# Causal attention computed for four heads at a time in 64-query blocks, instead of two heads in 128-query blocks

## The chip, the cores and the metric

The kernel runs on one core of one Trainium2 chip. The metric is the device time of one execution in microseconds (us). Three timed runs of the kernel before the change took 458.64, 459.05 and 459.47 us; their median, 459.05 us, is the time to compare with.

## The reference

There are 4 batches of 12 heads, 448 positions and head size 64, all in float32. The attention is causal; its output, laid out as rows of 768 channels, is the x of a mixing layer:

```python
scores = scale * np.matmul(q, k.transpose(0, 1, 3, 2))        # scale = 1/8
scores = np.where(mask, -1000000000.0, scores)                # mask: keys after the query
scores = scores - np.max(scores, axis=-1, keepdims=True)
attn = np.exp(scores)
attn = attn / (np.sum(attn, axis=-1, keepdims=True) + 1e-09)
out = np.matmul(attn, v)

theta = x @ w_theta                                            # x: 4 x 448 x 768
zr, zi = x * np.cos(theta), x * np.sin(theta)
y = np.einsum('ts,bsd->btd', w_tok_r, zr) + np.einsum('ts,bsd->btd', w_tok_i, zi)
u = x + y
result = u + np.maximum(u @ w_ch, 0.0)
```

## The kernel before

Attention is done pair by pair: 24 pairs of heads, six to a batch, each by one call of attend. TensorE (PE) computes the scores with the queries as stationary operand, 128 queries at a time. Queries 0 to 383 make three blocks of 128, whose keys reach to 128, 256 and 384. A head has only 64 channels, so the two heads of a pair use the two halves of the PE array's rows at the same time (line 627). The last 64 queries of both heads are put together into one block of 128 stationary columns, with zeros where one head's query meets the other's channels, and multiplied with all 448 keys on the full array (line 614). VectorE (DVE) adds the mask and takes the row's extreme (line 633), ScalarE (ACT) takes exp and the sums (line 636). PE then transposes the weights in 16 blocks of 128 by 128, in five groups of one PSUM bank each (line 671); ACT or DVE copies each group into the tile pt (lines 504 and 506). The product with v runs as two 128-row, 64-column halves of the array, one for each head, in four steps of 448, 320, 192 and 64 queries (line 697). The seven columns of sums of a pair are inverted on DVE, transposed by PE into the bank xo (line 646), copied (line 647), written to HBM and read back spread over 64 partitions (rb); DVE multiplies the product by rb into xT (line 700).

The rest is full-array work: theta (line 749), the sine and cosine of it, the token mixing y (line 828), and a channel product by a scheme with fewer multiplications (line 926). Weights are decoded on the chip first: ACT and DVE turn raw words into float32 (lines 528 to 534), then a rounded part and a rest are stored by a copy (lines 501 to 506) and a subtraction (line 512).

All instructions are put in order ahead of time by a planner (class Plan). Every piece of work has an engine, a duration that the planner assumes, buffers out of rings of fixed size, and a due time; two tables of numbers, SHIFT and PEN, move the due times of single groups of instructions. At each moment the planner gives a free engine the piece that is due first among those whose inputs and buffers are there; turn adds a duration where PE changes between full-array work and work on halves. What it emits is the order of each engine, and engines run strictly in that order, waiting on each other by semaphores. PSUM has eight banks: two of s, two of t, one xo, three of m. All DMAs are issued by SyncE's queue (line 487).

Of the kernel before, what the change touches and what calls it, by code (L numbers as in the profile page):

```python
# [8 lines left out]
F32 = mybir.dt.float32  # L9
# [12 lines left out]
KN = dict(S0=-62237.8965, P0=19471.4322, P1=5606.0978, V=2.9624, TL=1.1607, RL=-85717.1261, SL=3920.8889, SH=90531.9904,  # L22
# [6 lines left out]
          C0=-30018.6467, C1=-154978.281, C2=8845.5904, SW=32591.9015, HL=13, MP=6, PM=6837.6742, MR3=3.9427, WQ=2)  # L29


SHIFT = {2: -279, 3: -584, 4: 210, 5: 775, 6: 6, 7: -41, 8: 17, 9: 443, 10: -218, 11: 111, 12: -69, 13: 4, 14: -100,
# [146 lines left out]
class Plan:  # L179
# [67 lines left out]
    def order(self):  # L247
# [21 lines left out]
        def turn(a, b):  # L269
            if a == b:  # L270
                return 0
            if b == "r":
                return 87 if a == "x" else 288
            if b == "x":
                return 54 if a == "r" else 145
            if a == "r":
                return 120 if b == "t" else 108
# [11 lines left out]
        out = []  # L289
# [845 lines left out]
```

## Time and profile before

| | |
|---|---|
| median of the three timed runs | 459.05 us |
| span of the profiled execution, first to last instruction | 456.9 us |
| PE busy | 445.3 us, 97% |
| DVE busy | 371.5 us, 81% |
| ACT busy | 247.6 us, 54% |
| POOL busy | 47.0 us, 10% |
| TensorE clock granted, mean | 0.999 of full speed |

The profiled execution is known by its span alone; what lies around the span in a timed run is taken as the difference to the median, 2.15 us. A matmul's duration in the rows includes the time it takes to pass through the array, during which the next one already runs, so the price of a group of matmuls is read from its start to the start of the next group, not from its busy time. A float32 matmul stands as two records. PEld is the load of the stationary operand.

### The profile page before, as it was taken

The page shows a single profiled execution, that of the slowest core. Times are in us where ns is not written, and L with a number is a line of the kernel's source. Part 1 is how long each engine was busy: PE and PEld are TensorE (multiplying, and loading weights), DVE is VectorE, ACT ScalarE, POOL GpSimd, SP SyncE. Part 2 cuts the span into 40 slices and gives each one's busy share as a digit, 9 for nine tenths or more (in the row PEclk, how much of TensorE's full clock was granted, in tenths as well). Part 3 has the DMA queues.
Part 4 walks back from the last instruction along what each step waited for, and adds up shares of the span by engine and source line. Part 5 has one row for each costly group of instructions (what it writes and reads, how often), then busy time and mean ns, then how long its engine had stood idle before and what let it go on. Part 6 is the DMA issues. An engine that isn't in the chain of part 4 may idle for free.

```text
span 456.9 us, 7721 instructions
## 1 busy us (share of the span) xinstructions
PE 445.3 (97%) x2651; PEld 367.1 (80%) x2651; DVE 371.5 (81%) x974; ACT 247.6 (54%) x617; POOL 47.0 (10%) x46
## 2 busy tenths in 40 slices
PE   8988999999999999999999999999999999999996
PEld 3655566877777778898878898889999988998995
DVE  4999999869978878547988846987657999888796
ACT  5988878668796665327984214971134542212320
POOL 1213000000000001000000000030011330242330
PEclk9999999999999999999999999999999999999999
DMA  8877655322445546301042230032423322017023
GB/s 281 339 263 235 207 174 167 90 89 94 117 149 165 189 145 246 95 20 50 11 131 84 45 140 8 28 115 83 172 72 110 105 75 70 2 65 238 21 80 142
DMA packets 35415, 56.10 MB, mean 123 GB/s; under 512 B 11912, under 2 KB 26032, under 8 KB 35376
## 3 DMA queue, kind: packets, MB, share of 16 engines
q1 hardware_dynamic: 35376, 55.61, 37.4%
q8 instruction: 21, 0.34, 0.3%
q14 instruction: 18, 0.15, 0.1%
HBM read 42.34 MB, written 11.69 MB: 118 GB/s over the span
## 4 chain that ended last, share of the span: by engine, by line
PE 82%; DVE 11%; DMA 3%; ACT 2%; issue 1%; SPq 0%; ACTq 0%
PE y L828 20%; PE th L749 19%; PE cp L926 15%; PE xo L697 8%; PE t L671 7%; PE s L627 4%; PE s L614 3%; PE t L627 2%; PE xp L808 1%; DMA raw<-w_theta 1%; DMA kk<-k 1%; DVE e L633 1%; DVE zl L512 1%; DVE zw L534 1%; DVE zw L531 1%
## 5 line engine op out<-in xcount | busy, mean ns | idle before, releaser
L749 PE MATMUL th<-wth,xs 128*128 128x384 f32 x528 | 102.5, 342 | 0.1
L828 PE MATMUL y<-wtk,zh 128*128 128x448 f32 x336 | 101.7, 383 | 0.0
L749 PEld LDWEIGHTS th<-wth,xs 128*128 128x128 f32 x528 | 90.6, 188 | 4.4 <-issue 1.4
L636 ACT ACTIVATE e<-e,sm 128x384 f32<-128x384 f32 (+2 forms) x144 | 72.3, 503 | 39.1 <-DVE sm L633 38.3
L828 PEld LDWEIGHTS y<-wtk,zh 128*128 128x128 f32 x336 | 59.5, 189 | 6.9 <-issue 2.2
L828 PE MATMUL y<-wtk,zl 128*128 128x448 f32 x168 | 61.5, 366 | 0.0
L697 PE MATMUL xo<-pt,vs 128*64 128x448 f32 (+3 forms) x384 | 48.1, 387 | 0.8 <-DVE rs L647 0.8
L633 DVE CUSTOM_DVE_ANT_0 e<-s,mask 128x128 f32<-128x128 f32 (+1 forms) x96 | 38.0, 413 | 9.0 <-PE s L627 7.8
L671 PE MATMUL t<-ident,e 128*128 128x128 f32 x288 | 43.9, 276 | 1.4 <-ACT pt L504 0.9
L926 PE MATMUL cp<-ub,wth 128*128 128x448 f32 x207 | 44.4, 367 | 0.8 <-DVE ub L506 0.6
L697 PEld LDWEIGHTS xo<-pt,vs 128*64 128x64 f32 x384 | 24.9, 136 | 25.1 <-issue 14.6
L671 PEld LDWEIGHTS t<-ident,e 128*128 128x128 f32 x288 | 33.8, 141 | 13.1 <-issue 4.4
L926 PEld LDWEIGHTS cp<-ub,wth 128*128 128x128 f32 x207 | 38.6, 188 | 4.8 <-DVE ub L506 1.0
L504 ACT COPY pt<-t 128x384 f32<-128x384 f32 (+2 forms) x69 | 32.9, 497 | 10.2 <-PE t L671 9.8
L926 PE MATMUL cp<-ub,wa 128*128 128x448 f32 x162 | 36.0, 366 | 0.6 <-DVE u L960 0.6
L828 PEld LDWEIGHTS y<-wtk,zl 128*128 128x128 f32 x168 | 31.5, 188 | 2.8
L926 PEld LDWEIGHTS cp<-ub,wa 128*128 128x128 f32 x162 | 30.3, 188 | 3.2 <-DVE u L960 0.9
L506 DVE COPY pt<-t 128x384 f32<-128x384 f32 (+2 forms) x51 | 28.8, 569 | 2.5 <-PE t L671 2.1
L627 PE MATMUL s<-kk,qs 64*128 64x384 f32 (+1 forms) x192 | 27.0, 393 | 1.0 <-DMA kk<-k 0.9
L512 POOL TENSOR_TENSOR zc<-zc 128x384 f32<-128x384 f32 x4 | 4.1, 1014 | 231.3 <-DVE zc L534 213.3
L636 ACT ACTIVATION_READ_ACCUMULATOR e<-e,sm 128x1 f32 x144 | 27.2, 189 | 0.0
L627 PEld LDWEIGHTS s<-kk,qs 64*128 64x128 f32 x192 | 18.4, 191 | 10.9 <-DVE sm L633 2.3
(112 smaller groups left out, 685.9 us busy)
## 6 DMA issues: line engine op xcount, KB each, us to landing
qs<-q SPq DMA_DIRECT2D x24, 256.0 KB, 3.6
vs<-v SPq DMA_DIRECT2D x24, 256.0 KB
kk<-k SPq DMA_DIRECT2D x24, 224.0 KB, 3.2
raw<-w_theta SPq DMA_DIRECT2D x6, 768.0 KB, 4.1
raw<-w_ch SPq DMA_DIRECT2D x6, 768.0 KB
wd<-zc SPq DMA_DIRECT2D x6, 768.0 KB, 3.6
wf<-wd SPq DMA_DIRECT2D x24, 192.0 KB, 3.0
raw<-w_tok SPq DMA_DIRECT2D x7, 448.0 KB
```

Source lines behind the costliest of these rows:

```text
L504: alts.append((e, ac(n, 0 if psum else 1), lambda: nc.scalar.copy(out=o(), in_=i())))
L506: alts.append((e, dv(n) if psum else dv2(n), lambda: nc.vector.tensor_copy(out=o(), in_=i())))
L512: P.op([(e, gp(n) if e == "POOL" else dv(n), lambda e=e: ENG[e].tensor_tensor(out=o(), in0=a(), in1=b(), op=op)) for e in engs], r=r, w=w, ...
L614: nc.tensor.matmul(out=s.t[:, 0:S], lhsT=qp.t[:, MQ:KW], rhs=kp.t)
L627: nc.tensor.matmul(out=s.t[:, c0:c0 + w], lhsT=qp.t[own, 128 * i:128 * i + 128], rhs=kp.t[own, 0:w])
L633: P.op("DVE", dv(w) + 8, lambda m0=m0, c0=c0, w=w, s=s, e=e, c=c: nc.vector.tensor_tensor_reduce(out=e.t, in0=s.t[:, c0:c0 + w], in1=mask[ ...
L636: P.op("ACT", ac(w, 2.5), lambda e=e, c=c: nc.scalar.activation(out=e.t, in_=e.t, func=AF.Exp, scale=-1.0, bias=sm.t[:, 0, c:c + 1], accum ...
L671: nc.tensor.transpose(ps.t[:, 128 * n:128 * n + 128], e.t[:, c:c + 128], ident)
L697: nc.tensor.matmul(out=xo.t[64 * a:64 * a + 64, 128 * j:S], lhsT=vs.t[:, c:c + D], rhs=pt.t[:, a, slot(j):slot(j) + w], start=(j == 0), st ...
L749: nc.tensor.matmul(out=th.t[:, 0:HW], lhsT=l, rhs=wth[:, p, w2, c0:c0 + HW], start=(p == 0 and n == 0), stop=(p == KD - 1 and n == len(ops ...
L828: nc.tensor.matmul(out=y.t[:, 0:S], lhsT=l.t[:, c], rhs=wtk[:, c, w2], start=(c == 0 and n == 0), stop=(c == NTK - 1 and n == 2))
L926: nc.tensor.matmul(out=banks[m].t[:, 0:S], lhsT=wt()[:, c, w2, 128 * m:128 * m + 128], rhs=ub[c].t[:, a], start=(first and c == 0 and n == 0),
```

## The change

Attention is done for two pairs at a time, a quad of four heads: 12 calls of attend. The queries are cut into seven blocks of 64, block x with 64(x+1) keys. For one block four matmuls are issued, each with 64 channels and 64 stationary columns, so each takes a quarter of the array: head a of a pair takes the rows, pair i the columns. Both pairs of head a land in one bank, one on each half of its partitions. The zero-padded block of the last queries is gone. For the second head of a pair the key blocks (and the blocks of v) are laid out in reverse order, on the host; so the last block of the first head and the first of the second lie side by side in a tile, and one transposition takes both diagonal blocks. A quad has 28 transpositions, where two pairs had 32, in seven groups of one bank, eight copies where there were ten. The transposed weights go into two fixed tiles pta and ptb, one for each head of the pair; blocks of them that stay zero are cleared once by POOL. The sums of four heads are inverted, transposed and sent out together. The product with v is as before, once for each pair.

```diff
-KN = dict(... V=2.9624, ... MP=6, PM=6837.6742, MR3=3.9427, WQ=2)
+KN = dict(... V=0.0, ... MP=3, H0=0.0, H1=0.1, H2=0.2, H3=0.3, H4=0.4, H5=0.5, H6=0.6, PM=6837.6742, MR3=3.9427, WQ=2)
+EB = (2, 2, 2, 2, 2, 2, 2)
+SG = ((3, 2, 0), (5, 1), (4,), (6,))
+ROOM = (("s", "t", "s", "t"), ("s", "m", "s", "t"))
+QO = 15.0
+TURN = ((0, 0, 145, 288), (0, 0, 145, 288), (106, 56, 0, 87), (108, 120, 54, 0))
-SHIFT = {2: -279, 3: -584, 4: 210, 5: 775, 6: 6, 7: -41, 8: 17, 9: 443, 10: -218, 11: 111, 12: -69, 13: 4, 14: -100,
+SHIFT = {2: 99415, 3: 9107, 4: -2529, 5: -6011, 6: -4744, 7: -5690, 8: 36879, 9: -6000, 10: 1863, 11: 9305, 12: 767, 13:
...
-    rings = dict(one=10 ** 6, kk=4, qs=4, vs=4, sm=3, rs=2, rd=3, rb=3, xT=KN["XT"], pt=2, eT=3,
+    rings = dict(one=10 ** 6, kk=3, qs=3, vs=3, sm=2, rs=2, rd=2, rb=3, xT=KN["XT"], pta=1, ptb=1,
...
+        loads = [(t[i], src, i, lo, hi) for i in range(2) for t, src, lo, hi in ((QS[n], q, 0, 4 * D if n == 0 else S), (KS[n], k, 0, S))]
+        if n == 0:
+            loads += [(QS[n][i], q, i, 4 * D, S) for i in range(2)]
...
+        for gi, (g, room) in enumerate(zip(SG, ROOM[n < KN["MP"]])):
+            P.now = t0 + per * gi
+            ss = [buf(room, [128, 512]) for _ in range(2)]
...
+                for x, c in blocks:
+                    w = D * (x + 1)
+                    for a in range(2):
+                        own = slice(D * a, D * a + D)
+                        for i in range(2):
+                            nc.tensor.matmul(out=ss[a].t[D * i:D * i + D, c:c + w], lhsT=qp[i].t[own, D * x:D * x + D], rhs=kp[i].t[own, S - w:S] if a else kp[i].t[own, 0:w])
+            rd = kp + [(qp[i], x) for i in range(2) for x in g]
+            P.op("PE", c0 / 0.6 + QO * len(g), mm, rd, [(z, x) for z in ss for x in g], mode="q")
...
+        rp, rs, rd, rb = buf("xo", [2 * NS, 128]), buf("rs", [2 * NS, 128]), buf("rd", [4, S]), [buf("rb", [128, S]) for _ in range(2)]
...
+        groups = [(0, "A", [(0, x) for x in (1, 2, 3, 4)]), (1, "A", [(0, x) for x in (1, 2, 3, 4)]),
+                  (None, "J", [(j, 2 * j) for j in (2, 0, 3, 1)]),
+                  (0, "C", [(j, x) for j in (2, 0) for x in (5, 6)]), (1, "C", [(j, x) for j in (2, 0) for x in (5, 6)]),
+                  (0, "B", [(1, x) for x in (3, 4, 5, 6)]), (1, "B", [(1, x) for x in (3, 4, 5, 6)])]
...
+                for y, (j, x) in enumerate(blocks):
+                    c = D * x if a is None else 128 * j if a == 0 else 2 * D * (x - j)
+                    nc.tensor.transpose(ps.t[:, 128 * y:128 * y + 128], E[x].t[:, c:c + 128], ident)
...
+                        nc.tensor.matmul(out=xo.t[D * a:D * a + D, 128 * j:S], lhsT=vs[i].t[:, c:c + D], rhs=pt[a].t[:, i, D * SLOT[j]:D * SLOT[j] + w],
+                                         start=(j == 0), stop=(j == NM))
```

What this does to the order of the engines is shown at three places. The first is PE in the stretch in which theta of the first batch is woven between attention: L627 and L614 are scores (L638 after), L671 transpositions, L646 the sums (L660 after), L697 products (L713 after), L749 theta (L766 after); x2 counts equal neighbours. Before, one pair:

```order
L671 MATMUL t<-ident,eT 128x128 x4
L646 MATMUL xo<-ident,sm 7x128
L749 MATMUL th<-wth,xs 128x384 x9
L697 MATMUL xo<-pt,vs 64x448 x2
L697 MATMUL xo<-pt,vs 64x320 x2
L697 MATMUL xo<-pt,vs 64x192 x2
L697 MATMUL xo<-pt,vs 64x64 x2
L627 MATMUL t<-kk,qs 128x256 x2
L627 MATMUL s<-kk,qs 128x384 x2
L627 MATMUL s<-kk,qs 128x128 x2
L749 MATMUL th<-wth,xs 128x384 x6
```

and after, the products of one pair of a quad and the scores of the next quad:

```order
L713 MATMUL xo<-pta,vs 64x448
L713 MATMUL xo<-ptb,vs 64x448
L638 MATMUL s<-kk,qs 64x320 x4
L638 MATMUL t<-kk,qs 64x384 x4
L638 MATMUL t<-kk,qs 64x128 x4
L713 MATMUL xo<-pta,vs 64x320
L713 MATMUL xo<-ptb,vs 64x320
L713 MATMUL xo<-pta,vs 64x192
L713 MATMUL xo<-ptb,vs 64x192
L713 MATMUL xo<-pta,vs 64x64
L713 MATMUL xo<-ptb,vs 64x64
L766 MATMUL th<-wth,xs 128x384 x6
```

Scores now come in fours, and groups of them can stand between the steps of one product; a product's steps are as they were.

The second place is the start of SyncE's queue, the first loads. Before:

```order
L487 DMA qs<-q 128x512
L487 DMA kk<-k 128x448
L487 DMA vs<-v 128x512
L487 DMA qs<-q 128x512
L487 DMA kk<-k 128x448
L487 DMA vs<-v 128x512
```

and after:

```order
L498 DMA kk<-k 128x448 x2
L498 DMA qs<-q 128x256 x2
L498 DMA qs<-q 128x448
L498 DMA qs<-q 128x192 x2
L498 DMA vs<-v 128x512 x3
L498 DMA kk<-k 128x448
L498 DMA raw<-w_theta 128x1536 x2
```

The first scores need two loads before and four after.

The third place is DVE around a product's multiplication (L700, after L716), while w_tok is decoded: L531 and L534 (after L542, L545) are decoding, L506 (after L517) stores the rounded part of it, L512 the rest. Before:

```order
L531 TENSOR_SCALAR zw<-raw 128x448 x2
L700 TENSOR_TENSOR xT<-xo,rb 128x448
L534 SCALAR_TENSOR_TENSOR zw<-zw 128x448
L643 TENSOR_SCALAR sm<-sm 128x7
L728 TENSOR_SCALAR xs<-xT 128x128
L647 COPY rs<-xo 7x128
L645 RECIPROCAL sm<-sm 128x7
L732 SCALAR_TENSOR_TENSOR xs<-xT,xs 128x128
L506 CAST wtk<-zw 128x448
L732 SCALAR_TENSOR_TENSOR xs<-xT,xs 128x128
L512 TENSOR_TENSOR wtk<-zw,wtk 128x448
```

and after:

```order
L716 TENSOR_TENSOR xT<-xo,rb 128x448
L542 TENSOR_SCALAR zw<-raw 128x448
L745 TENSOR_SCALAR xs<-xT 128x128
L542 TENSOR_SCALAR zw<-raw 128x448
L661 COPY rs<-xo 14x128
L749 SCALAR_TENSOR_TENSOR xs<-xT,xs 128x128 x2
L545 SCALAR_TENSOR_TENSOR zw<-zw 128x448
L542 TENSOR_SCALAR zw<-raw 128x448
L517 CAST wtk<-zw 128x448
L542 TENSOR_SCALAR zw<-raw 128x448
```

The subtraction for wtk stands on DVE seven times before and once after; the other six are on POOL now.

## Rows read from the trace of the kernel before

**Rows 1.** The page: busy time, share of the span, instructions of three engines.
```profile
PE 445.3 (97%) x2651; PEld 367.1 (80%) x2651; DVE 371.5 (81%) x974; ACT 247.6 (54%) x617; POOL 47.0 (10%) x46
```

**Rows 2.** Windows: stretch, its length, busy us of each engine, clock, DMA share, GB/s.
```profile
10.00:60.00 50.00, 45.88 (x291) 29.37 (x292) 48.50 (x165) 42.44 (x126) 8.12 (x5) 1.00 0.74 253
60.00:350.00 290.00, 289.66 (x1821) 241.97 (x1818) 225.07 (x623) 168.63 (x422) 10.44 (x10) 1.00 0.34 109
350.00:400.00 50.00, 49.07 (x249) 44.13 (x248) 47.93 (x89) 19.63 (x36) 11.61 (x10) 1.00 0.22 62
400.00:457.00 57.00, 52.33 (x264) 47.83 (x262) 46.53 (x79) 12.28 (x22) 14.68 (x12) 0.99 0.32 109
```

**Rows 3.** Timeline of PE, one pair's work: start us, us, instruction, count.
```profile
141.06 1.95 PE L697 MATMUL xo<-pt,vs 128*64 128x448 f32 x16
142.94 0.70 PE L627 MATMUL t<-kk,qs 64*128 64x256 f32 x4
143.48 1.03 PE L627 MATMUL s<-kk,qs 64*128 64x384 f32 x8
144.44 0.67 PE L828 MATMUL y<-wtk,zh 128*128 128x448 f32 x2
...
145.16 0.49 PE L671 MATMUL t<-ident,e 128*128 128x128 f32 x3
145.49 0.92 PE L614 MATMUL s<-kk,qs 128*128 128x448 f32 x2
146.24 0.60 PE L671 MATMUL t<-ident,e 128*128 128x128 f32 x4
```

**Rows 4.** Line L627 and line L697: duration ns min/median/max of records.
```profile
L627 PE MATMUL t<-kk,qs x72: 376/377/480, 57.9 to 283.8; 64*128 64x256 f32 x72
...
L697 PE MATMUL xo<-pt,vs x384: 219/405/591, 18.2 to 297.8; 128*64 128x448 f32 x48, 128*64 128x320 f32 x48, 128*64 128x192 f32 x48, 128*64 128x64 f32 x48
```

**Rows 5.** Chain of waits, three pieces in order: start us, us, what.
```profile
128.04 1.23 PE y L828 x6
...
133.16 0.87 PE s L627 x8
134.02 1.42 PE y L828 x6
```

**Rows 6.** Timeline of the start: first scores, first DVE work, second pair's scores.
```profile
4.28 1.67 PE L627 MATMUL s<-kk,qs 64*128 64x384 f32 x8
...
6.10 0.56 DVE L633 CUSTOM_DVE_ANT_0 e<-s,mask 128x384 f32<-128x384 f32 x1 [5.08 <-PE s L627]
...
8.22 1.14 PE L627 MATMUL s<-kk,qs 64*128 64x384 f32 x8 [0.89 <-DMA kk<-k]
```

**Rows 7.** DMA issues: KB each.
```profile
qs<-q SPq DMA_DIRECT2D x24, 256.0 KB, 3.6
vs<-v SPq DMA_DIRECT2D x24, 256.0 KB
kk<-k SPq DMA_DIRECT2D x24, 224.0 KB, 3.2
```

**Rows 8.** Timeline of DVE around the sixth pair's multiplication (L700).
```profile
67.70 0.42 DVE L633 CUSTOM_DVE_ANT_0 e<-t,mask 128x256 f32<-128x256 f32 x1
...
68.05 0.42 DVE L633 CUSTOM_DVE_ANT_0 e<-t,mask 128x256 f32<-128x256 f32 x1
...
68.42 0.63 DVE L512 TENSOR_TENSOR wtk<-zw,wtk 128x448 fp32r<-128x448 f32 x1
68.96 0.28 DVE L633 CUSTOM_DVE_ANT_0 e<-s,mask 128x128 f32<-128x128 f32 x1
...
71.10 0.62 DVE L700 TENSOR_TENSOR xT<-xo,rb 128x448 f32<-128x448 f32 x1
```

**Rows 9.** Waits: who waited for whom, us in total, times, longest us.
```profile
PE t L671 <- ACT pt L504: 2.0, 5, 0.6
```

More of the change, by code (lines that the diff above doesn't have):

```diff
@@ L19 @@
 MAGIC = 12582912.0
-KN = dict(S0=-62237.8965, P0=19471.4322, P1=5606.0978, V=2.9624, TL=1.1607, RL=-85717.1261, SL=3920.8889, SH=90531.9904,
+KN = dict(S0=-62237.8965, P0=19471.4322, P1=5606.0978, V=0.0, TL=1.1607, RL=-85717.1261, SL=3920.8889, SH=90531.9904,
           LD=12898.2959, LW=-112284.387, M0=22282.9249, MR=2.3734, MR2=2.348, W0=-8106.6576, WT=34569.4757,
@@ L28 @@
           QM=88138.2839, AS=2003.9869, XD=-44653.8104, ER=36496.8626, LF=-52786.1393, O1=-8635.2897, O2=165141.793,
-          C0=-30018.6467, C1=-154978.281, C2=8845.5904, SW=32591.9015, HL=13, MP=6, PM=6837.6742, MR3=3.9427, WQ=2)
-SHIFT = {2: -279, 3: -584, 4: 210, 5: 775, 6: 6, 7: -41, 8: 17, 9: 443, 10: -218, 11: 111, 12: -69, 13: 4, 14: -100,
[101 rows of a table removed]
-PEN = {4: -70, 6: -295, 8: 1312, 10: -508, 12: 351, 16: 1398, 18: -136, 20: 4, 22: -103, 24: 246, 26: 652, 28: 1588,
[28 rows of a table removed]
+          C0=-30018.6467, C1=-154978.281, C2=8845.5904, SW=32591.9015, HL=13, MP=3, H0=0.0, H1=0.1, H2=0.2, H3=0.3, H4=0.4, H5=0.5, H6=0.6, PM=6837.6742, MR3=3.9427, WQ=2)
+EB = (2, 2, 2, 2, 2, 2, 2)
[4 more added lines that the diff above has]
+SHIFT = {2: 99415, 3: 9107, 4: -2529, 5: -6011, 6: -4744, 7: -5690, 8: 36879, 9: -6000, 10: 1863, 11: 9305, 12: 767, 13:
[113 rows of a table added]
+PEN = {4: 14105, 6: -5988, 8: -17504, 10: -1225, 12: -4027, 14: -5212, 16: 10353, 18: -857, 20: 29527, 22: 9693, 24:
[27 rows of a table added]
 class Buf:
@@ L269, in turn @@
         def turn(a, b):
[L270 to L277, printed above, removed]
-            if a == "x":
-                return 56 if b == "t" else 106
-            return 0
+            return TURN["mtxq".index(a)]["mtxq".index(b)]
         n_free = dict(self.rings)
@@ L407, in attention_moe_kernel @@
     MQ = 128 * NM
-    KW = MQ + 2 * TAIL
-    PW = 3 * (MQ - TAIL) + S
+    NS = S // D
+    NQ = NP // 2
+    PW = 18 * D
+    SLOT = (3, 13, 0, 10)
     HW = DM // 2
@@ L423, in attention_moe_kernel @@
     o_pool = []
-    rings = dict(one=10 ** 6, kk=4, qs=4, vs=4, sm=3, rs=2, rd=3, rb=3, xT=KN["XT"], pt=2, eT=3,
+    rings = dict(one=10 ** 6, kk=3, qs=3, vs=3, sm=2, rs=2, rd=2, rb=3, xT=KN["XT"], pta=1, ptb=1,
                  s=2, t=2, xo=1, m=3, R=2, C=2, xs=2, kq=2, xd=2, zh=2, zl=2, none=1)
-    for i in range(NM):
-        rings[f"e{i}"] = 3
+    for i in range(NS):
+        rings[f"e{i}"] = EB[i]
     rings.update(ub=6, q1=1, ot=2, wf=2)
@@ L455, in attention_moe_kernel @@
     ident = const.tile([128, 128], F32, name="ident")
-    mask = const.tile([128, MQ + S], F32, name="mask")
+    mask = const.tile([128, 2 * S - D], F32, name="mask")
+    pts = [apool.tile([128, 2, PW], F32, name=n, tag=n) for n in ("pta", "ptb")]
     halfpi = const.tile([128, 1], F32, name="halfpi")
@@ L585, in attention_moe_kernel @@
     QS, KS, VS = {}, {}, {}
-    def load_pair(pr):
-        b, p = divmod(pr, NP)
-        t0 = tau(2 * pr)
-        kp, qp = buf("kk", [128, S]), buf("qs", [128, KW])
-        dma(lambda: [(kp.t, k[b, p])], (1, 229376), [], [kp], pr=t0 - KN["LD"])
-        dma(lambda: [(qp.t, q[b, p])], (1, 262144), [], [qp], pr=t0 - KN["LD"] + 1, row=2048)
-        KS[pr], QS[pr] = kp, qp
-        vs = buf("vs", [128, 8 * D])
-        dma(lambda: [(vs.t, v[b, p])], (1, 262144), [], [vs], pr=t0 - KN["LD"] + 1000, row=2048)
-        VS[pr] = vs
@@ L703, in tails, with load_quad @@
-    def tails(t):
-        return t[:, :, 2 * TAIL:].rearrange("p a (j c) -> p j a c", j=4)[:, :, :, MQ - 2 * TAIL:]
+    def load_quad(n):
+        b, u = divmod(n, NQ)
+        t0 = tau(4 * n)
+        KS[n], QS[n], VS[n] = [], [], []
+        for i in range(2):
+            KS[n].append(buf("kk", [128, S]))
+            QS[n].append(buf("qs", [128, S]))
+        loads = [(t[i], src, i, lo, hi) for i in range(2) for t, src, lo, hi in ((QS[n], q, 0, 4 * D if n == 0 else S), (KS[n], k, 0, S))]
+        if n == 0:
+            loads += [(QS[n][i], q, i, 4 * D, S) for i in range(2)]
+        for c, (t, src, i, lo, hi) in enumerate(loads):
+            w = [(t, x) for x in range(NS) if lo <= D * x < hi] if src is q else [t]
+            dma(lambda t=t, src=src, i=i, lo=lo, hi=hi: [(t.t[:, lo:hi], src[b, 2 * u + i, :, lo:hi])], (1, 512 * (hi - lo)), [], w,
+                pr=t0 - KN["LD"] + c, row=4 * (hi - lo))
+        for i in range(2):
+            vs = buf("vs", [128, 8 * D])
+            dma(lambda vs=vs, i=i: [(vs.t, v[b, 2 * u + i])], (1, 262144), [], [vs], pr=t0 - KN["LD"] + 1000, row=2048)
+            VS[n].append(vs)
@@ L706, in attention_moe_kernel, with strided @@
+    def strided(t, u, y, z):
+        t = t[:, :, D * u:D * u + D]
+        return bass.AP(tensor=t.tensor, offset=t.offset, ap=[t.ap[0], t.ap[1], [D * y, 2], [D * z, 2], [1, D]])
     th_last = []
@@ L1010, in consts @@
         nc.gpsimd.memset(mask, 0.0)
-        for own, c, n in ((slice(0, 128), MQ, 128), (slice(0, 64), MQ + S, 64), (slice(64, 128), MQ + S, 64)):
-            nc.gpsimd.affine_select(out=mask[own, c - n:c], in_=mask[own, c - n:c], pattern=[[-1, n]],
+        for own in (slice(0, D), slice(D, 128)):
+            nc.gpsimd.affine_select(out=mask[own, S - D:S], in_=mask[own, S - D:S], pattern=[[-1, D]],
                                     compare_op=ALU.is_ge, fill=-8e9, base=0, channel_multiplier=1)
+        for h in range(2):
+            own = slice(D - D * h, 128 - D * h)
+            nc.gpsimd.memset(strided(pts[h][own], 0, 10, 3), 0.0)
     def warm():
@@ L1031, in attention_moe_kernel @@
     for b in range(B):
-        for p in range(NP):
-            load_pair(NP * b + p)
-            attend(NP * b + p)
+        for u in range(NQ):
+            load_quad(NQ * b + u)
+            attend(NQ * b + u)
         if b == B - 1:
@@ L1101, in _lay_out @@
     qp, kp = _pairs_t(q), _pairs_t(k)
-    zero = np.zeros_like(qp[:, :, :d, m:])
-    qp = np.concatenate([np.concatenate([qp[:, :, :d], zero], axis=3),
-                         np.concatenate([qp[:, :, d:, :m], zero, qp[:, :, d:, m:]], axis=3)], axis=2)
     vp = v.reshape(b, h // 2, 2, s, d)
-    vm = vp[:, :, :, :m].reshape(b, h // 2, 2, 3, 128, d).transpose(0, 1, 4, 3, 2, 5).reshape(b, h // 2, 128, 6 * d)
-    vt = vp[:, :, :, m:].transpose(0, 1, 3, 2, 4).reshape(b, h // 2, s - m, 2 * d)
-    vt = np.concatenate([np.zeros_like(vt), vt], axis=2)
+    vp = np.concatenate([vp, np.zeros_like(vp[:, :, :, :128 * (s // 128 + 1) - s])], axis=3)
+    vp = vp.reshape(b, h // 2, 2, s // 128 + 1, 2, 64, d)
+    vp = np.stack([vp[:, :, 0], vp[:, :, 1, :, ::-1]], axis=2).reshape(b, h // 2, 2, s // 128 + 1, 128, d)
+    vp = vp.transpose(0, 1, 4, 3, 2, 5).reshape(b, h // 2, 128, 2 * d * (s // 128 + 1))
+    kp = kp.reshape(b, h // 2, 2, d, s // 64, 64)
+    kp = np.stack([kp[:, :, 0], kp[:, :, 1, :, ::-1]], axis=2).reshape(b, h // 2, 2 * d, s)
     arrays = {
@@ L1111, in _lay_out @@
         "k": kp,
-        "v": np.concatenate([vm, vt], axis=3),
+        "v": vp,
         "w_theta": inputs["moe_w_theta"].reshape(dm // 128, 128, dm),
```

167 lines of the change are left out of this document (73 added, 94 removed), and 269 rows, old and new, of tables (PEN, SHIFT).

## The prediction

> **What bounds the kernel now.** First the page's busy times: PE is busy 97% of the span, DVE 81%, ACT 54% [rows 1]. A mean hides stages, so next the windows [rows 2]: from 60 to 350 us PE has no gap worth the name (289.66 of 290) while DVE stands at 225 of 290, so there every microsecond of PE work is a microsecond of time. From 10 to 60 us it is different: DVE is busy 48.50 of 50, PE 45.88, and busy PE counts matmuls that stretch while they pass through the array. The reader is to see two stages, a short one that DVE paces and a long one that PE paces. In the last 107 us PE misses 5.6 us, mostly behind the last additions. Third, PE's timeline of one pair [rows 3] gives the prices that the sum needs, from start to start.
>
> **The scores.** Before, a pair has three groups of scores. From 142.94 to 143.48, 0.54 us, for 256 columns of both heads; to 144.44, 0.96 us, for 384 and 128; and 145.49 to 146.24, 0.75 us, for the last queries on the full array [rows 3]. Sum 2.25 us, 24 times 54.0 us. The full-array group has 448 columns in 0.75 us, 1.67 ns a column; by that the two half-array groups would take 0.43 and 0.855 us, so each carries 0.11 us more, for loading first weights and for emptying the array when the mode changes. That the two heads really run side by side is in the durations: four records of 0.377 us within 0.54 us, and sixteen of 0.405 us (median) within the 1.88 us of a product [rows 3, 4]. The first are halves by rows, the second halves by columns. Nothing in the trace shows both cuts at once, which is what the change uses.
>
> If four quarters run side by side, a quad costs what its longest stream costs: 64 times (1+2+...+7) = 1792 columns, 2.99 us, and 35.9 us for twelve. Four groups a quad at 0.11 us add 5.3 us: 41.2 us. The lower bound would be fewer entries, as neighbours in the order share one (28 entries, 3.1 us: 39.0). The upper bound comes from the density: a quad's 28 matmuls are 56 records, which must follow each other at 0.061 us to fit into 2.99 + 0.44 us. The nearest spacing that rows show is the transpositions', 0.33 us for three, 0.11 us [rows 3]; at that a quad would take 6.2 us and all of them 74 us. I take 41.2, since the two records of a side-by-side pair already start together and the 0.11 us of a transposition is spent on one full 128-column load each, which a quarter does not need. Gain 12.8 us, between -20 (a loss) and 15.
>
> **Transpositions and sums.** 48 transpositions fewer (4 a quad) and 12 transpositions of sums fewer, 60 at 0.11 us [rows 3]: 6.6 us. All are on PE, so all count in the long stage. The eight copies are off the path as far as rows show: PE waited 2.0 us in all for one [rows 9].
>
> **Modes.** Counted in the order of before, PE returns to full-array work 37 times after halves; after, 27 times. Such a return costs its follower: six y matmuls take 1.42 us right behind scores and 1.23 us elsewhere [rows 5], of which 0.11 is in the scores' price already. Ten times 0.1 us: 1 us. Entries into products go from 30 to 28, nothing. The products keep their 24 times 1.88 us.
>
> So PE's work falls by 12.8 + 6.6 + 1.0 = 20.4 us.
>
> **What of it is lost at the start.** The first scores need both pairs' k (224 KB each) and the first halves of both q (128 KB each), 704 KB, where one q and one k, 480 KB, were enough [rows 7]. Before, those 480 KB let PE start at 4.28 us; the second pair's k, last of 1216 KB in issue order, let its scores start at 8.22 [rows 6]. In between lies 704 KB at 4.28 + 3.94 x 224/736 = 5.5 us: 1.2 us later. Queued behind are all of DVE's masks, whose first one stood at 6.10 us; it paces this stage, so they are late by as much. Bounds: 0, since the second pair is then at hand earlier, and 4 us, if all four loads came only with the last at 8.22.
>
> Then DVE's work ahead of the sixth pair's multiplication, which stood at 71.10 us [rows 8]. Counted in the two orders up to there: masks 59 with 16512 columns, then 56 with 14336, at 0.35 us for 256 (0.08 and one column a nanosecond): 2.5 us less. Copies 14, then 7, of about 0.5 us for near twice the columns: 2.5 us less. Of decoding w_tok (448 columns, 0.54 us a full-rate pass) six subtractions, three shift-and-or passes, six half-word passes of about 0.3 us and one cast go elsewhere or later: 7 us less. Two casts of w_theta more, 1.0; eleven to thirteen small operations on sums fewer, 1.6 us less. Sum 12.6 us less. PE's work up to there, counted likewise: 31 transpositions fewer (3.4), scores 13.7 for 19.0 us (5.3), three transposed sums (0.3), nine theta matmuls at 0.18 us later (1.6), and some 3 us of mode changes: 13 to 14 less. DVE and PE shrink alike, so PE's idle time ahead of it (70 us less some 60 of work at the same prices, 10 us) grows by the later start of 1.2 us and about 1 us that DVE gives back less: 2 us. The new joint read of the sums is a wait too: pair 0 of a quad can be multiplied only when the seven blocks of all four heads are summed, sent and back; behind it on DVE stand the masks of the next quad, and on PE the second product, which needs the one bank xo. In the first quad PE has nothing else to put between the two products and in the second 0.9 us; later ones have 1.3 us or more by the order, against 0.62 for a multiplication [rows 8].
>
> **Sum.** 456.9 - 20.4 + 2 = 438.5 us of span. The median of the timed runs lies 2.15 us above the span: 440.6, say 440 us. Over the whole run DVE loses about 10 us of 371 (a quad has 384 mask columns less, 0.4 us, and half as many small operations on sums, 0.4 us), so in the long stage its share rises from 78% to about 80%, no bound.
>
> **A rule that speaks against it.** The trace shows nothing denser than a full-array matmul each 0.11 us over a longer stretch [rows 3]. The Trainium skill, TensorE: Matmul & The Clock Gate, Part 1 (The HAM clock gate), says that where matmuls are decoded in microcode the sequencer spends about 62 ns on each, and that this becomes the bound once the array needs less. By that an estimate for a quad is 56 x 0.062 + 0.44 = 3.9 us, 5.8 us more for all, and 446 us. Whether it holds here no row can tell.
>
> **Rivals.**
> *Matmuls can't be issued so densely.* For it: only spacings of 0.11 us and more are in the rows. Against it: pairs of records start together. At spacings from 0.07 to 0.085 us, on the way from what is needed to what is shown, a quad takes 0.5 to 1.3 us more: 446 to 456 us.
> *The quarters don't run side by side, or only as densely as transpositions.* Place: every group of scores. If two columns of a row half go one after the other, a quad costs twice 2.99 us, 36 us more: 476 us, and by the spacing of 0.11 us 473 us: slower. Decided where a quad's scores cost 1.55 us over the 3.43 of the forecast. Against it: each cut alone works, and so do two streams from the same partitions in a product [rows 4].
> *The order leaves waits.* pta and ptb exist once, so all of a quad's products must end before the next quad's copies start, and xo is one bank. Speaks for it: the start. Against: between the last product of a quad and the first of the next the order has 5.7 us of PE work or more, the transpositions among it. At 0.5 to 1.2 us a quad: 446 to 454.
> *The start gets better, not worse.* Six w_tok subtractions go to POOL, which had 8 of 50 us busy [rows 2]; if DVE's idle head costs nothing, PE loses 4 to 8 us less: 432 to 436.
>
> **Chances.** The forecast (436 to 445) 0.64; better start 0.09; denser issue fails 0.09; waits 0.10; quarters fail 0.08. What can be told from no change is 0.2%, 0.9 us. Faster 0.90 (the first four cases, less a little for waits that eat all), same 0.02, slower 0.08. The range that leaves out the failing quarters and the far ends is 431 to 453.
>
> **What would show it.** In the profile after: scores as four records that start together, a group of 512 columns in about 0.96 us, 1792 columns in about 3.4; transpositions still 0.11 us apart, 336 of them; PE at 99% from 60 us on; the first score near 5.5 us, DVE nearly full to 55 us, the sixth multiplication near 60. I am wrong if the four records of a block follow one another, if PE shows idle time ahead of products, or if DVE ends the waits beyond 60 us.

## The result, and the profile after

The changed kernel takes 442.49 us (median of four runs, 441.3 to 445.56) against 459.26 (458.64 to 459.49): ratio 0.9645, 95% interval 0.9607 to 0.9682. Forecast were 440.0 us and 431 to 453. The profiled execution took 441.63 us, its span is 439.8. In a second comparison the same kernel took 442.0 us (span of the profiled run 440.2), ratio 0.963 (0.9607 to 0.9654); the experiments below are held against that one.

The busy times, as in [rows 1]:

```profile
PE 425.3 (97%) x2927; PEld 354.3 (81%) x2927; DVE 358.7 (82%) x928; ACT 241.8 (55%) x602; POOL 55.1 (13%) x48
```

PE's busy time falls by 20.0 us and the span by 17.1; DVE loses 12.8. The windows, as in [rows 2] (length, busy us of PE, PEld, DVE, ACT, POOL, granted clock, DMA share, GB/s):

```profile
10.00:60.00 50.00, 43.15 (x392) 28.36 (x386) 46.24 (x164) 43.39 (x134) 10.95 (x7) 0.93 0.73 243
60.00:344.00 284.00, 283.22 (x2036) 238.11 (x2034) 227.68 (x608) 168.50 (x410) 16.81 (x11) 1.00 0.36 114
344.00:384.00 40.00, 38.96 (x196) 35.41 (x196) 34.88 (x58) 13.28 (x27) 12.20 (x10) 1.00 0.20 58
384.00:440.00 56.00, 51.70 (x262) 47.70 (x261) 47.55 (x84) 13.43 (x24) 12.27 (x10) 1.00 0.31 111
```

From 60 us on PE is as full as before, and DVE, at 80%, is no bound. New is the first row's clock, 0.93 where it was 1.00, and DVE's 46.24 of 50 us. PE's timeline of one quad's scores and products, to be held against [rows 3]:

```profile
91.56 0.59 PE L713 MATMUL xo<-pta,vs 128*64 128x448 f32 x1
...
93.44 1.09 PE L638 MATMUL t<-kk,qs 64*64 64x384 f32 x16
94.36 1.05 PE L638 MATMUL s<-kk,qs 64*64 64x256 f32 x24
95.34 0.59 PE L713 MATMUL xo<-pta,vs 128*64 128x448 f32 x1
...
97.22 0.98 PE L638 MATMUL t<-kk,qs 64*64 64x448 f32 x8
98.02 0.72 PE L638 MATMUL s<-kk,qs 64*64 64x320 f32 x8
98.67 2.38 PE L766 MATMUL th<-wth,xs 128*128 128x384 f32 x12
```

From start to start the four groups of scores take 0.92, 0.98, 0.80 and 0.65 us, 3.35 in all; over the eight quads past 60 us the mean is 3.42 (forecast 3.43). Each product still takes 1.88 (91.56 to 93.44). Next the start, in finer windows:

```profile
5.00:10.00 5.00, 4.68 (x44) 3.67 (x48) 2.15 (x15) 1.88 (x9) 0.00 (x0) 1.00 0.95 283
10.00:16.00 6.00, 2.31 (x27) 1.22 (x19) 5.86 (x22) 5.73 (x20) 0.39 (x1) 1.00 1.02 405
16.00:20.00 4.00, 3.40 (x36) 2.23 (x39) 2.91 (x6) 1.88 (x5) 1.61 (x1) 0.57 0.52 197
20.00:27.00 7.00, 6.69 (x65) 3.69 (x57) 6.86 (x30) 6.77 (x24) 1.82 (x1) 1.00 0.51 145
27.00:30.00 3.00, 0.75 (x10) 0.37 (x8) 3.00 (x10) 3.00 (x9) 0.09 (x1) 1.00 0.75 237
30.00:35.00 5.00, 4.99 (x36) 3.36 (x33) 2.62 (x10) 2.40 (x8) 1.72 (x1) 0.66 0.98 344
```

Twice PE is idle most of the time (from 10 to 16 and from 27 to 30 us), and right behind each its clock stands at the low level of 1.2 GHz for the larger part of a row (means of 0.57 over 4 us and 0.66 over 5), in which PE is busy and DVE idles for 1.1 and 2.4 us. What PE waited for between 10 and 60 us (total, times, longest):

```profile
PE t L683 <- ACT e L650: 3.2, 2, 1.7
PE xo L713 <- DVE xT L716: 2.3, 1, 2.3
PE t L683 <- DVE pta L517: 1.1, 1, 1.1
```

And DVE's sixth multiplication, which stood at 71.10 us [rows 8]:

```profile
61.84 0.61 DVE L716 TENSOR_TENSOR xT<-xo,rb 128x448 f32<-128x448 f32 x1
```

### The profile page after: what moved, and what is told of

It reads as the page before. It is cut to its first block, busy times and chain, and to the rows that moved or that the text cites. A ratio compares the mean times of both kernels' runs of the same rounds, so it can differ in the third digit from the quotient of the medians.

```text
span 439.8 us, 8190 instructions
## 1 busy us (share of the span) xinstructions
PE 425.3 (97%) x2927; PEld 354.3 (81%) x2927; DVE 358.7 (82%) x928; ACT 241.8 (55%) x602; POOL 55.1 (13%) x48
## 4 chain that ended last, share of the span: by engine, by line
PE 86%; DVE 9%; DMA 2%; issue 1%; ACT 1%; SPq 0%; DVEq 0%; ACTq 0%
PE y L845 22%; PE th L766 20%; PE cp L943 15%; PE xo L713 10%; PE t L683 8%; PE s L638 4%; PE t L638 4%; PE xp L825 2%; DVE e L647 2%; DMA raw<-w_theta 1%; DMA qs<-q 1%; DVE R L788 1%; DVE C L828 1%; DVE zw L542 1%; DVE zl L523 1%
## 5 line engine op out<-in xcount | busy, mean ns | idle before, releaser
L766 PE MATMUL th<-wth,xs 128*128 128x384 f32 x528 | 106.1, 344 | 0.0
L766 PEld LDWEIGHTS th<-wth,xs 128*128 128x128 f32 x528 | 90.1, 188 | 5.2 <-issue 3.3
L650 ACT ACTIVATE e<-e,sm 128x64 f32<-128x64 f32 (+6 forms) x168 | 83.3, 498 | 17.5 <-DVE sm L647 17.3
L713 PE MATMUL xo<-pta,vs 128*64 128x448 f32 (+1 forms) x192 | 48.8, 394 | 2.3 <-DVE xT L716 2.3
L713 PE MATMUL xo<-ptb,vs 128*64 128x448 f32 (+1 forms) x192 | 48.8, 394 | 0.0
L683 PEld LDWEIGHTS t<-ident,e 128*128 128x128 f32 x336 | 39.5, 143 | 10.8 <-issue 2.4
L713 PEld LDWEIGHTS xo<-pta,vs 128*64 128x64 f32 x192 | 24.4, 139 | 27.3 <-issue 14.9
L943 PE MATMUL cp<-ub,wth 128*128 128x448 f32 x207 | 45.1, 366 | 0.0
L943 PEld LDWEIGHTS cp<-ub,wth 128*128 128x128 f32 x207 | 38.8, 188 | 3.1
L647 DVE CUSTOM_DVE_ANT_0 e<-s,mask 128x64 f32<-128x64 f32 (+3 forms) x96 | 31.2, 366 | 10.2 <-PE s L638 10.0
L943 PE MATMUL cp<-ub,wa 128*128 128x448 f32 x162 | 37.0, 366 | 0.0
L523 POOL TENSOR_TENSOR ub<-xT,ub 128x448 fp32r<-128x448 f32 x5 | 12.0, 2402 | 180.2 <-DVE ub L517 170.6
L845 PEld LDWEIGHTS y<-wtk,zl 128*128 128x128 f32 x168 | 31.5, 188 | 2.9
L943 PEld LDWEIGHTS cp<-ub,wa 128*128 128x128 f32 x162 | 30.2, 188 | 2.2
L650 ACT ACTIVATION_READ_ACCUMULATOR e<-e,sm 128x1 f32 x168 | 31.5, 188 | 0.0
L647 DVE CUSTOM_DVE_ANT_0 e<-t,mask 128x448 f32<-128x448 f32 (+2 forms) x60 | 27.3, 498 | 0.8 <-PE t L638 0.5
L515 ACT CAST ub<-tt 128x448 fp32r<-128x448 f32 x19 | 10.6, 567 | 30.2 <-PE cp L943 17.0
L638 PE MATMUL s<-kk,qs 64*64 64x64 f32 (+3 forms) x384 | 24.7, 368 | 1.1 <-DMA qs<-q 1.0
```

The lines of the kernel that those rows point to most:

```text
L515: alts.append((e, ac(n, 0 if psum else 1), lambda: nc.scalar.copy(out=o(), in_=i())))
L523: P.op([(e, gp(n) if e == "POOL" else dv(n), lambda e=e: ENG[e].tensor_tensor(out=o(), in0=a(), in1=b(), op=op)) for e in engs], r=r, w=w, ...
L638: nc.tensor.matmul(out=ss[a].t[D * i:D * i + D, c:c + w], lhsT=qp[i].t[own, D * x:D * x + D], rhs=kp[i].t[own, S - w:S] if a else kp[i].t[ ...
L647: P.op("DVE", dv(w) + 8, lambda a=a, c=c, w=w, y=y, e=e, s=ss[a]: nc.vector.tensor_tensor_reduce(out=e.t[:, w * a:w * a + w], in0=s.t[:, c ...
L650: P.op("ACT", ac(w, 2.5), lambda a=a, w=w, y=y, e=e: nc.scalar.activation(out=e.t[:, w * a:w * a + w], in_=e.t[:, w * a:w * a + w], func=A ...
L683: nc.tensor.transpose(ps.t[:, 128 * y:128 * y + 128], E[x].t[:, c:c + 128], ident)
```

## The experiments

Theory: the gain is TensorE's work, above all four score streams side by side, and past the sixth multiplication the time follows that work one to one. Rival: it comes from the new order and the relief on DVE. A second dispute concerns the start, which gives back more than forecast: is it the idle waits and the low clock, DVE's work, the loads, or the one bank xo? This table has a row for each run; the last three columns are from its profiled execution. "Last stretch" runs from the first matmul of the channel product behind the last one of y (L943 of the changed kernel) to the last matmul, the same instructions in all these kernels.

| run | median us | sixth mult. | tenth mult. | last stretch |
|---|---|---|---|---|
| changed kernel / again | 442.49 / 442.0 | 61.8 / 62.6 | 107.3 / 107.7 | 62.2 / 62.2 |
| a1_warm | 443.58 | 61.4 | 107.4 | 63.4 |
| a2_bridge | 441.9 | 60.4 | 106.6 | 63.4 |
| a3_bank | 442.05 | 61.2 | 106.2 | 63.4 |
| b1_joint_twice | 447.99 | 63.5 | 109.5 | 62.2 |
| b2_rows_only | 448.7 | 65.2 | 111.3 | 63.4 |
| b3_cols_only | 447.89 | 63.8 | 110.0 | 63.4 |
| c1_bank_bridge | 441.46 | 62.3 | 108.1 | 63.4 |
| d1_two_streams | 482.46 | 79.1 | 129.9 | 62.2 |
| d2_less_dve | 441.68 | 60.8 | 106.1 | 62.2 |
| d3_early_k | 444.8 | 64.8 | 110.1 | 62.2 |
| e1_theta_later_bank | 443.81 | 62.9 | 108.1 | 63.4 |

### The gain: how many streams, and TensorE's work

**b2_rows_only and b3_cols_only.**

```diff
-                for x, c in blocks:
-                    for a in range(2):
-                        for i in range(2):
+                for i in range(2):        # b2; in b3: for a in range(2):
+                    for x, c in blocks:
+                        for a in range(2):    # b3: for i in range(2):
```

> The same score matmuls in another order inside a group: first all blocks of the pair in columns 0 to 63 with both row halves, then all of the pair in columns 64 to 127; so two quarters at a time share the array, cut by rows, instead of four. Theory that the scores gained by four streams side by side: a quad's scores cost twice 2.99 us instead of once, 36 us more in all, some of it hidden in the head's waits: 469 to 478. Rival, the cut by columns adds nothing (the gain is elsewhere): 442.

> As the run before, but first all blocks of row half 0 with both column halves, then all of row half 1: two quarters at a time, cut by columns. By the theory of four streams as long as the cut by rows, 469 to 478; longer than it by 3 us or more if two quarters on the same rows get in each other's way when their weights are loaded. Rival, the cut by rows adds nothing: 442.

Measured 448.7 us (two runs, 447.28 and 450.12) and 447.89 (447.02 and 448.76): 6.7 and 5.9 us more, not 27 to 36. Both theories missed. The timeline of b2_rows_only says why:

```profile
97.04 1.11 PE L638 MATMUL t<-kk,qs 64*64 64x384 f32 x16
97.96 1.53 PE L638 MATMUL s<-kk,qs 64*64 64x256 f32 x24
99.42 0.59 PE L713 MATMUL xo<-pta,vs 128*64 128x448 f32 x1
...
101.30 0.98 PE L638 MATMUL t<-kk,qs 64*64 64x448 f32 x8
102.10 0.72 PE L638 MATMUL s<-kk,qs 64*64 64x320 f32 x8
102.75 2.36 PE L766 MATMUL th<-wth,xs 128*128 128x384 f32 x12
```

Groups of one or two blocks take the same 0.92, 0.80 and 0.65 us in any issue order; only the group of three blocks grows, from 0.98 to 1.46 (in b3_cols_only too). Twelve times 0.48 us is 5.8. These rows fit one reading: a quarter that is busy takes a further matmul into waiting, and the issue goes on to the next quarter; it stops only at a third matmul for the same quarter. In the single records of that group the fifth one of 256 columns, which can only be of the other column half (each half has four), starts at 98.40 us, before the first of 64 columns, which was issued ahead of it (98.72). Strictly in the emitted order, as the description of the kernel before has it, these matmuls don't start. The Trainium skill, TensorE: Matmul & The Clock Gate, Part 3 (The mechanism), says that matmuls start strictly in program order; by this trace they do not where they lie on different quarters. The two runs thus didn't take the streams apart, and another was needed.

**d1_two_streams.**

```diff
-                        own = slice(D * a, D * a + D)
+                        own = slice(0, D)
```

> The scores of the second head of each pair are computed from the first head's rows (so the output isn't attention of all heads): both use row half 0, and only two of the four quarters of the array work, with as many matmuls of the same lengths and the same order. The two reorderings before cost 6 us and not 36, because a quarter that is busy holds a further matmul and the issue goes on to the others; here no issue order can help. Theory that the scores gained by four streams side by side: a quad's scores take 6.3 instead of 3.35 us; 35 us in all, of which the nine quads after the sixth multiplication count in full, 27: 469 to 477. Rival, two streams already fill what the array can do: 442 to 446.

Measured 482.46 us (482.38 and 482.54), ratio 1.0507 (1.0465 to 1.0549) to the kernel before: slower than that.

```profile
113.41 1.94 PE L638 MATMUL t<-kk,qs 64*64 64x384 f32 x16
115.19 1.91 PE L638 MATMUL s<-kk,qs 64*64 64x256 f32 x24
117.03 0.59 PE L713 MATMUL xo<-pta,vs 128*64 128x448 f32 x1
...
118.91 1.72 PE L638 MATMUL t<-kk,qs 64*64 64x448 f32 x8
120.46 1.24 PE L638 MATMUL s<-kk,qs 64*64 64x320 f32 x8
121.63 2.38 PE L766 MATMUL th<-wth,xs 128*128 128x384 f32 x12
```

A quad's scores take 1.78 + 1.84 + 1.55 + 1.17 = 6.34 us, 2.99 more, as expected, 36 us for all. Four quads' scores, and not three, stand ahead of the sixth multiplication in the trace. Behind it, to the last matmul, the run takes 24.0 us more than a0_again, and eight times 2.99 is 23.9. The sixth multiplication itself comes 16.5 us later; four quads' scores are 12.0 of it, and 4.5 are lost besides in the head, where TensorE's matmuls took twice their later durations up to 36 us (last section). So four streams do share the array, and two alone would have made the change a loss.

**b1_joint_twice.**

```diff
-                for y, (j, x) in enumerate(blocks):
+                for y, (j, x) in list(enumerate(blocks)) * (2 if a is None else 1):
```

> Every joint group of four transpositions is issued twice (the second writes the same numbers over the first): 48 transpositions more, as many as the change took away, on TensorE alone; the order stays. Theory, TensorE's work is what the time follows: 4 x 0.109 = 0.44 us a quad, 5.2 us for twelve, of which the three quads ahead of the sixth multiplication may hide some in TensorE's waits: 3.9 to 5.2 us over the 442.0 of the changed kernel, 446 to 447. Rival, the gain of the change came from the new order and from fewer operations on DVE: under 1 us.

Measured 447.99 us (447.73 to 449.1), 6.0 more; 0.9 of it lies ahead of the sixth multiplication (63.5 for 62.6). TensorE's work counts in full, at 0.125 us a transposition, and the rival (under 1 us) falls. What the new order, with its new tables in the planner, brings by itself no run shows.

### The start: edits of the first quad

**a0_again**, the yardstick.

> The changed kernel itself, once more, as the yardstick for the three small edits run beside it: 0.9645 of the kernel before by the first comparison, so 442 to 443 us. Both theories say the same.

Measured 442.0 us (five runs, 440.87 to 442.65).

**a1_warm.**

```diff
-        for _ in range(KN["NW"]):
-            P.op("PE", 854, lambda: nc.tensor.matmul(... 256 columns of zeros ...), [], [y])
+        for n in range(KN["NW"]):
+            P.op("PE", 854, lambda n=n: idle(1, 256) or (n == KN["NW"] - 1 and idle(1, 352)), [], [y])
```

> One warm-up matmul of 352 columns more (1.17 us at the spacing of the other four), so that TensorE isn't idle from 4.15 us to the first score at 5.32. In the changed kernel the first score groups run from 5.3 to about 9.6 us at twice the later durations (256 columns in 0.44 us a record against 0.21). Theory that the clock costs time at the start: the clock rises near 5 us, as it did before, the first mask on DVE comes at about 6.8 instead of 7.85, and as DVE is full from there the whole time falls by about 1 us. Rival, that this head costs nothing because DVE and the DMAs set the pace later: DVE's first masks come earlier, but the end moves by less than 0.3 us.

**a2_bridge.**

```diff
                 for y, (j, x) in enumerate(blocks):
+                    if n == 0:
+                        idle({(0, 0): 3, (0, 3): 3, (2, 0): 2}.get((gn, y), 0))
```

> Eight matmuls of zeros (0.43 us each at the high clock) into the warm-up's bank, in three places where TensorE waits for the first quad's exponentials and copies: three ahead of the first transposition, three ahead of the fourth, two ahead of the joint ones; in all 3.4 of 4.3 us of idle time. Theory that the clock costs time: the granted clock stays at 1.00 through 16 to 20 us, where it was 0.63 and 0.52, 3.3 us of TensorE's work there take half as long, DVE no longer sits idle between 17 and 20 us, and the whole time falls by 1 to 1.7 us. Rival, the stage is DVE's: under 0.3 us. If a matmul of zeros stands in the way of a transposition that was ready, up to 0.4 us slower each.

**a3_bank.**

```diff
+            to = second if n == 0 and i else xo     # second: the bank of the first quad's second m tile
-                def pv(i=i, j=j, w=w, xo=xo):
+                def pv(i=i, j=j, w=w, xo=to):
```

> In the first quad alone the second pair's product goes into a score bank that is free by then instead of the one bank xo, so that it needn't wait for the first pair's multiplication; nothing else moves. Theory that the wait for the bank costs time: the product starts at about 27.3 instead of 29.42 us, the half clock of 30.2 to 33.6 us goes or shortens, and the time falls by 1 to 2 us. Rival, the wait only moves: TensorE's next transpositions need exponentials whose masks DVE reaches at 30.3 us, so TensorE waits there instead, its clock falls all the same, and the time moves by less than 0.5 us.

The three measured 443.58 us (442.15 to 444.91), 441.9 (441.63 to 442.49) and 442.05 (441.64 to 442.46): the first 1.6 us slower, of which its last stretch has 1.2, the other two the same. The edits did what they should. In a1_warm the first mask came at 7.09 us, but then PE waited, and its granted clock was 0.64 from 10 to 16 us and 0.50 from 16 to 20. In the profiled execution of a2_bridge the granted clock stayed at 1.00 throughout:

```profile
10.00:16.00 6.00, 4.17 (x22) 1.83 (x21) 4.99 (x16) 4.80 (x16) 0.30 (x1) 1.00 1.00 388
16.00:20.00 4.00, 3.86 (x55) 2.54 (x54) 3.48 (x11) 2.48 (x7) 1.71 (x1) 1.00 0.65 198
```

In a3_bank the second product started at 27.6 instead of 29.4 us (31.5 in a0_again), and PE waited 5.7 us for exponentials, where it had been 3.2 (4.2 in a0_again):

```profile
PE t L685 <- ACT e L652: 5.7, 4, 2.4
PE t L685 <- DVE pta L517: 0.7, 1, 0.7
```

Up to the tenth multiplication a2_bridge is ahead of a0_again by 1.1 us and a3_bank by 1.5, but their last stretch took 1.2 us longer, for a cause that lies elsewhere (last section; the 0.7 in the expectation below is counted from DVE's last addition of y, which started 0.5 us later in a2_bridge). Nor is the lead shown to be the edits': in both executions the first scores already ran at their later durations and the first mask came at 7.01 and 7.24 us, for 7.85 and 8.01 in the two of the changed kernel, though neither edit touches anything ahead of it (last section). The medians show no gain from either edit; what idle time and low clock cost in the head they leave open. Both together:

> Both edits of the first quad at once: the second product in a free score bank, and eight matmuls of zeros where TensorE waits. Singly they brought the tenth multiplication from 107.7 to 106.6 and 106.2 us, and the last stretch then took 0.7 to 1.3 us longer, at 0.207 us a matmul instead of 0.203. If the head's gains add up, the tenth multiplication comes at 105 to 105.5 and the time falls by 1 to 2.5 us; if they lift the same wait, it comes near 106 and the time stays within 0.5 us of the changed kernel.

**c1_bank_bridge**: 441.46 us (440.52 to 445.09), the same. In its profiled execution the first mask came at 7.90 us and the tenth multiplication at 108.1. But that execution took 443.81 us, one of the two longest of six; the other four took 440.52 to 442.01. Whether the two edits add up is not shown.

**d2_less_dve.**

```diff
+        c = slice(0, 64 if wh and n == DM else n)
-            out=f().bitcast(I32), in0=f().bitcast(I32), scalar=3, in1=g(), op0=ALU.logical_shift_left,
+            out=f().bitcast(I32)[:, c], in0=f().bitcast(I32)[:, c], scalar=3, in1=g()[:, c], op0=ALU.logical_shift_left,
```

> The shift-and-or pass that decodes w_theta on DVE does only 64 of 768 columns (so the weights are wrong): DVE has 6 x 0.8 = 4.8 us less work ahead of about 45 us, TensorE as much as before. If DVE's work paces the head, the sixth multiplication comes 3 to 4.5 us earlier than 61.8 to 62.6, and the time falls by as much. If the chain from score over mask, exponential, transposition and copy to the product paces it, or the DMAs, under 1.5 us.

Measured 441.68 us (440.32 to 443.1). DVE is busy 43.17 us between 10 and 60 instead of 46.24 (45.73 in a0_again), and the sixth multiplication comes 1.0 to 1.8 us earlier, at 60.8: less than the 3 to 4.5 of the theory. DVE's work alone doesn't pace the head; the first step of the prediction had said that it does.

**d3_early_k.**

```diff
+                if n == 0 and src is k:
+                    return [(t.t[0:D, 0:256], g[0:D, 0:256]), (t.t[D:128, S - 256:S], g[D:128, S - 256:S])]
...
-                nc.sync.dma_start(out=f[0], in_=f[1])
+                (nc.scalar if any(f[2:]) else nc.sync).dma_start(out=f[0], in_=f[1])
```

> The first quad's loads in another cut: of each k only the 256 columns that the first score group needs (128 KB instead of 224), the rest behind the second halves of q, and the two first halves of q issued by ACT beside SP's. 512 KB instead of 704 ahead of the first score. If the later first score costs time, it comes at about 4.5 instead of 5.3 us, the first mask at 6.0 to 6.8 instead of 7.85, and the time falls by 1 to 1.7 us. If what paces the head is met later (loads of w_theta, waits for exponentials), the first mask comes earlier and the time moves by less than 0.5 us.

Measured 444.8 us (443.88 to 447.08), ratio 0.9694 (0.9664 to 0.9724) to the kernel before: 2.8 us slower than the changed kernel, though the first score came at 4.28 us and the first mask at 6.26. The waits between 10 and 60 us:

```profile
PE t L692 <- ACT e L659: 4.3, 2, 4.1
...
ACT zw L539 <- DMA raw<-w_theta: 2.8, 1, 2.8
```

ACT decodes w_theta's first block between two exponentials; it stood 2.8 us for the load of it and began at 15.77 us instead of 12.70, and PE stood 4.1 us for the exponential behind. That the loads in more pieces pushed this block back is the likely reason, not tested apart. The last run took this decoding out of the way:

**e1_theta_later_bank.**

```diff
+    a, d = queue["ACT"], queue["DVE"]
+    a[9:13] = a[10:13] + a[9:10]
+    d[15:23] = d[20:22] + d[15:17] + d[22:23] + d[17:20]
```

> In the changed kernel ACT's decoding of the first w_theta block (0.9 us, and it waits for that block's load) stands between the exponentials of e1 and e4, and DVE's six passes on the first two blocks stand ahead of the first copies into pta and ptb. Here ACT does it behind e4, and DVE behind the two copies; besides, the second product of the first quad goes into a free score bank, as in a run before. Theory that the head is paced by the chain score, mask, exponential, transposition, copy, product, and by loads that wait in its way: TensorE's wait for e4 (1.5 to 4.1 us, at 13 to 17 us of the runs so far) falls to under 1 us, the sixth multiplication comes at 59.5 to 60.5 instead of 61.2 to 62.6, the tenth at 105 to 106, and the time falls by 1 to 2.5 us against the changed kernel. Rival, the waits only move to the next thing that is late (the second quad's loads, the sums' way through memory): less than 0.5 us, as with all the other edits of the head.

Measured 443.81 us (440.96 to 445.13): not faster. A wait had come up at the sums, whose reciprocal stands on DVE behind the passes that were put back:

```profile
PE xo L662 <- DVE sm L661: 2.9, 2, 2.6
PE t L685 <- ACT e L652: 2.9, 4, 1.7
PE t L685 <- ACT pta L515: 1.7, 1, 1.7
```

But the edit brought a cost of its own. Of the passes on w_theta the two ahead of the reciprocal took 2.68 us, where two others took 1.10, with a subtraction on POOL beside them; the planner holds such a pass back while POOL works, and the reordered queue no longer does:

```profile
15.30 1.10 DVE L542 TENSOR_SCALAR zw<-raw 128x768 uint16<-128x768 uint16 x2
18.33 2.68 DVE L542 TENSOR_SCALAR zw<-raw 128x768 uint16<-128x768 uint16 x2
20.91 0.22 DVE L661 RECIPROCAL sm<-sm 128x14 f32<-128x14 f32 x1
```
```profile
18.57 1.98 POOL L523 TENSOR_TENSOR wth<-zw,wth 128x768 fp32r<-128x768 f32 x1 [14.91 <-DVE wth L517]
```

So this run doesn't settle what the decoding is worth.

No version is shown to be faster than the changed kernel.

## Why the prediction was right, step by step

**What bounds.** Right from 60 us on. In the head wrong: I let DVE pace it. There each engine in turn waits for another in a chain of score, mask, exponential, transposition, copy and product, with loads in between, and where a link was taken away (bank, first load, decoding) a longer wait stood at another; no edit of the head brought the median down clear of the noise.

**Scores.** Mechanism right (d1_two_streams), and the size too: 3.42 us a quad in the mean past 60 us for 3.43, a gain of 54.0 - 41.0 = 13.0 us for 12.8. The quad shown above, at 3.35, is a cheap one. The rival of issue too dense falls: 24 records follow each other in 0.98 us, 41 ns apart. The Trainium skill, TensorE: Matmul & The Clock Gate, Part 1 (The HAM clock gate), has some 62 ns a matmul where hardware decode is off; counted by records, as the prediction did, the trace doesn't agree. Counted by whole matmuls of two records it is 82 ns, which doesn't test the rule; which decoding runs here no row tells.

**Transpositions.** Right: 336 remain, and 48 more cost 6.0 us where 5.2 were counted (b1_joint_twice).

**Modes.** The count holds in the traces (37 returns to full-array work before, 27 after). Its 1.0 us was not tested apart; that a change has a price shows in the group of three blocks past 60 us, which takes 0.92 us where scores follow, 0.98 where a product does and 1.02 in the mean where full-array work does.

**The start.** This term was mis-sized. The sixth multiplication was to come 11.1 us earlier, at 60; it came 9.3 and 8.5 us earlier. So the start cost some 4 us and not 2. Foreseen were the first score (5.32 us for 5.5) and the second product's wait for the bank (2.3 us); not foreseen were the low clock and the waits for exponentials. The prediction priced all work in the head as it is later, at the high level, and put the clock at nothing. The execution of a2_bridge, at the high level from the first score on, reached the sixth multiplication at 60.4 us, the earliest of those with all the work in place, which points to the clock; but c1_bank_bridge, low at the first scores and then at 1.00 until past 30 us, came at 62.3. How the 2 us divide among these, and which order would win them back, stays open.

**After it.** From the sixth multiplication to the last matmul the kernel before took 382.0 us, the changed one 374.1 and 373.7: 7.9 and 8.3 us less, for 7.3 forecast. So the head's 1.8 and 2.6 us too much are made up in part by 0.6 and 1.0 us more behind it; spans of 439.8 and 440.2 us against 438.5 are what remains. That much of the closeness is luck. The scores don't explain the surplus (0.01 us a quad); the transpositions at 0.125 for 0.11 us would make some 0.3 us of it (an estimate from b1_joint_twice; by the traces 22 of the 60 lie behind the sixth multiplication, where the prediction's count left 26); the rest stays open.

**Waits in later quads** (pta and ptb single, one bank xo): none; 0.8 us of 284 are idle between 60 and 344 us.

## What to carry over

Where one engine is full, count its work from start-to-start times, and trust the sum; where several are nearly full in turn, an idle time seen in the trace is no price: here none of the edits that removed one brought the median down clear of the noise. Cutting a matmul with 64 channels and 64 columns of weights into quarters paid here with four independent streams and lost with two, and a quarter that got a third matmul before the others had theirs cost 0.48 us a group. Before crediting an edit with a microsecond of one profiled execution, see whether the two executions started at the same level of the clock and ended at the same pace.

## What was not expected of the hardware

The granted clock stands in the row of 5 to 10 us as 1.00, yet the first group of three blocks took one quarter 1.73 us (5.32 to 7.05), where it takes 0.98 later. The durations stay double up to 9.6 us:

```profile
5.32 2.21 PE L638 MATMUL s<-kk,qs 64*64 64x256 f32 x18 [0.96 <-DMA qs<-q]
7.05 0.95 PE L638 MATMUL t<-kk,qs 64*64 64x448 f32 x1
```

In a2_bridge, whose instructions are the same up to there, that group took 1.15 us (in a3_bank 1.16), though PE had been idle for longer ahead of it, 1.31 us for 0.96:

```profile
5.38 1.39 PE L638 MATMUL s<-kk,qs 64*64 64x256 f32 x18 [1.31 <-DMA qs<-q]
6.53 0.59 PE L638 MATMUL t<-kk,qs 64*64 64x448 f32 x1
```

And in d1_two_streams the clock's row from 5 to 36 us says 1.00 too, while eight transpositions in it take nearly twice what they take later:

```profile
31.38 1.97 PE L683 MATMUL t<-ident,e 128*128 128x128 f32 x8
...
43.70 1.09 PE L683 MATMUL t<-ident,e 128*128 128x128 f32 x8
```

So at the start of an execution the durations tell the low level where the clock's row doesn't, and the level at the first scores differs between executions of the same instructions.

The last stretch is a nearly uninterrupted stream, mostly of 448-column matmuls, and it ran at one of two paces: 0.2026 or 0.2067 us from start to start, kept from the last wait to the end, with the granted clock at 1.00 in both. The same 40 us of the changed kernel and of a3_bank:

```profile
380.00:420.00 40.00, 40.00 (x199) 37.07 (x198) 34.02 (x62) 11.72 (x21) 9.61 (x8) 1.00 0.30 104
```
```profile
380.00:420.00 40.00, 40.00 (x195) 36.34 (x194) 34.16 (x62) 11.73 (x21) 9.62 (x8) 1.00 0.30 104
```

199 and 195 records run in the same time. Over the stretch that is 1.2 us, about as much as the edits of the head could win. Of fourteen profiled executions seven had the short pace (the kernel before and both of the changed one among them) and seven the long one. Whether the program, or the moment at which the last wait ends, decides it was not tried.
